# A plain group of chunks 8 to 11 opens the third batch, and ScalarE's queue loads q and k of the later rounds

## The chip, the core and the metric

The program runs on one core of a Trainium2 chip. The time is device time in microseconds (us), from the first to the last instruction of one execution; lower is better. Engines: TensorE (PE, with its weight loads PEld), VectorE (DVE), ScalarE (ACT), GpSimd (POOL) and SyncE (SP), which only issues transfers.

## What is computed

Eight batches of 576 tokens with 512 features go through three layers, all in float32. First linear attention with 8 heads of 64:

```python
q_s = softmax(q, over the head's 64 features)
k_s = softmax(k, over the 576 tokens)
x = q_s @ (k_s.T @ v)                      # per batch and head
```

Then a layer norm and a feed-forward layer with 2048 hidden values, `x + relu(norm(x) @ w_ch1) @ w_ch2`, and last a causal attention with four experts, of which each token uses two. The change touches the first two layers only.

## The kernel before

Everything is held with features on the partitions and tokens along the rows, in two halves of T = 288 tokens (h = 0, 1). TensorE multiplies in a rounded format, so every operand is split into a high and a low part (`split`: the high part by ScalarE, the remainder by VectorE), and a product takes three matmuls (high x high, high x low, low x high).

**Attention.** A *unit* is one pair of heads of one batch: 32 units, four per batch. `a_unit` runs one in six steps: the maxima of k and q (`km`, `sm`), the transposed maximum of k (`pkm`), the exponents (`ke` on ScalarE, `qe` on GpSimd), the transposes of q (`pq`), the product of k and v (`pkv`), and the result (`po`), copied to `xT`. Units run ahead of the feed-forward layer: while batch b is multiplied, the units of batch b + 1 are worked on. q and k of a unit live in two buffers each, so unit n + 2 is loaded when unit n has used its own: k behind `k_exp` (L495 on), q behind the second `q_scale` (L510 on), v behind `kv_product`, all by SyncE's queue.

**Feed-forward.** The 2048 hidden values are 16 chunks of 128 (f = 0 to 15); chunks 0 to 11 are multiplied in this phase, 12 to 15 later. Batches 0 and 1 run plain: `Step.first` multiplies one chunk (12 matmuls into `psh`), `high`/`low` take the relu into `hh`, and `Step.rest`, one step later, adds it into four sums (`acc`). From the third batch on (`FAST = 2`), the chunks go in three groups of four (`fast_group`, 0 to 3, 4 to 7, 8 to 11). The normalised input is cut into four blocks: b11 and b21 are the two halves of the features of the first half of the tokens, b12 and b22 those of the second half. Each group makes its products from seven blocks, b11, b22, b21 and four differences: t1 = b12 - b11, t2 = b22 - t1, t3 = b12 - b22, t4 = b21 - t2 (made by GpSimd, then split). `XORD` is the order in which the products use them. One product is 12 matmuls (`pa`, `pb`, `pc`), a group 84, against 96 in the plain form; after a group, `second` adds its four hidden chunks to the sums (96 matmuls). The weights of the seven products (`w_r`) come from a table in HBM (`w_d`) that is made during batch 1: `Sums` forms sums of weight blocks and stores them by ScalarE's queue, 5 stores for each of six pairs of chunks.

**What sets the order.** The loops hand work out in slots: a batch's steps or pieces are cut into a number of slots, and each slot calls some step of a unit (every `UNIT_GAP` slots a unit begins), of a norm (`NORM_AT`), of the blocks (`Mix.part`, `Mix.send` which stores a block for later) or of `Sums`. The tile framework then puts each engine's instructions in an order of its own by when it takes their inputs to be ready, and each engine and each queue runs its list strictly in that order. Each transfer also waits for an earlier one that used the same of eight semaphores.

In the last slots of batch 1, the norm of the third batch's two halves runs (`layer_norm`, sums `pmu` and `pvar`); then `first_space` and `last_space` give out buffers for the seven blocks and `hid` (hidden values), and the third batch starts with its first seven-product group.

## Time and profile before

| | |
|---|---|
| median of three runs | 1344.47 us (1344.16 to 1349.64) |
| profiled execution | 1343.84 us |
| its span | 1341.8 us |
| TensorE busy | 1295.0 us (97%) |
| VectorE, ScalarE, GpSimd busy | 979.2, 738.4, 403.0 us |

Times below are microseconds from the start of the span. Batch 1 is multiplied from about 160 to 247, the third batch from there to about 350, the following four batches in 86 to 87 us each, and the last batch of this phase to 793. `psh`, `acc`, `pa`, `pb`, `pc` are the sums in PSUM of the feed-forward layer, `pkm`, `pkv`, `pq`, `po` those of the attention units; `xm`, `xw_a`, `xw_b` hold the seven blocks; `xc` is the centred input. TensorE's granted clock is given as a share of its full speed of 2.4 GHz; the lower level is 1.2.

### The profile page before, as it was taken

How to read it: one execution, taken by the hardware profiler on the slowest of the kernel's cores; microseconds unless marked ns; L12 is line 12 of the kernel's file. 1: busy time of each engine (PE TensorE's matmuls, PEld its weight loads, DVE VectorE, ACT ScalarE, POOL GpSimd, SP SyncE). 2: the span in 40 equal slices, each digit the busy share in tenths (PEclk: the TensorE clock that was granted, in tenths of full speed). 3: DMA queues.
4: the chain of work that ended last, by engine and by line, in shares of the span. 5: the costliest groups of instructions: out<-in, count | busy, mean ns of one | idle time of the engine just before them, and what ended most of it. 6: DMA issues, size and time to landing. Idle time of an engine off the chain costs nothing.

```text
span 1341.8 us, 27486 instructions
## 1 busy us (share of the span) xinstructions
PE 1295.0 (97%) x9907; PEld 1244.7 (93%) x9907; DVE 979.2 (73%) x2776; ACT 738.4 (55%) x1884; POOL 403.0 (30%) x496
## 2 busy tenths in 40 slices
PE   6999999799999999999999999999999999999998
PEld 5789989699899998999999999999999999999996
DVE  6885766868869778787577457787777777777774
ACT  5875435545445554544445235656565665666665
POOL 6676245333233322342225002112121112121222
PEclk9999999799999999999999999999999999999999
DMA  9763377665756758656367224333323242333122
GB/s 238 225 210 102 114 236 259 219 178 185 243 181 224 219 197 261 201 200 184 127 248 234 72 72 134 91 102 86 107 76 106 80 107 94 91 107 91 45 50 74
DMA packets 173414, 203.52 MB, mean 152 GB/s; under 512 B 93152, under 2 KB 137696, under 8 KB 170976
## 3 DMA queue, kind: packets, MB, share of 16 engines
q1 hardware_dynamic: 150656, 164.80, 41.2%
q10 hardware_dynamic: 22624, 36.97, 7.6%
q8 instruction: 79, 1.29, 0.4%
q14 instruction: 55, 0.45, 0.1%
HBM read 140.13 MB, written 46.40 MB: 139 GB/s over the span
## 4 chain that ended last, share of the span: by engine, by line
PE 77%; DVE 9%; DMA 5%; ACT 2%; issue 1%; SPq 1%; POOL 0%; DVEq 0%; ACTq 0%; POOLq 0%
PE acc L191 18%; PE psh L191 11%; PE psqk L191 7%; PE psc L191 7%; PE pa L194 6%; PE pssc L191 4%; PE py L191 4%; PE pso L191 4%; PE psv L191 4%; PE pc L194 3%; PE pst L1842 3%; DMA q<-in_q_dram 2%; PE po L191 1%; PE pb L194 1%; DVE km L453 1%
## 5 line engine op out<-in xcount | busy, mean ns | idle before, releaser
L191 PE MATMUL psh<-xhl,w 128*128 128x288 f32 x1248 | 190.4, 300 | 1.3 <-DVE xhl L712 1.0
L191 PEld LDWEIGHTS psh<-xhl,w 128*128 128x128 f32 x1248 | 174.2, 190 | 4.0 <-DVE xhl L712 1.5
L1825 POOL TENSOR_SCALAR sm<-sm,st,lg 128x128 f32<-128x128 f32 (+3 forms) x128 | 81.8, 649 | 264.9 <-DVE lg L1742 63.0
L191 PE MATMUL acc<-xw_a,w 128*128 128x288 f32 x912 | 130.6, 297 | 3.2 <-DVE xT L1404 3.2
L191 PE MATMUL acc<-hid,w 128*128 128x288 f32 x912 | 128.0, 297 | 3.6 <-DVE tmp L1341 3.6
L191 PEld LDWEIGHTS acc<-hid,w 128*128 128x128 f32 x912 | 123.0, 188 | 5.0 <-DVE tmp L1341 4.5
L191 PEld LDWEIGHTS acc<-xw_a,w 128*128 128x128 f32 x912 | 123.4, 188 | 4.5 <-DVE xT L1404 4.2
L191 PE MATMUL psqk<-x,wqk 128*128 128x288 f32 x768 | 112.9, 297 | 0.4 <-DVE k L1645 0.4
L191 PEld LDWEIGHTS psqk<-x,wqk 128*128 128x128 f32 x768 | 105.1, 188 | 1.6 <-PE pst L1842 0.6
L191 PE MATMUL psc<-hb,w 128*128 128x288 f32 x672 | 100.2, 298 | 0.0
L1404 DVE TENSOR_TENSOR xT<-xT,acc 128x288 f32<-128x288 f32 x152 | 66.9, 445 | 40.0 <-PE acc L191 39.4
L1813 ACT ACTIVATE sm<-sm,st 128x128 f32<-128x128 f32 (+3 forms) x144 | 83.9, 584 | 20.9 <-DVE st L1805 19.3
L191 PE MATMUL acc<-hh,w 128*128 128x288 f32 x576 | 89.2, 303 | 3.8 <-ACT hh L806 2.2
L191 PEld LDWEIGHTS psc<-hb,w 128*128 128x128 f32 x672 | 92.1, 188 | 0.3
L191 PEld LDWEIGHTS acc<-hh,w 128*128 128x128 f32 x576 | 80.4, 190 | 6.4 <-ACT hh L806 2.9
L1866 ACT ACTIVATE aTh<-pst 128x128 fp32r<-128x128 f32 (+4 forms) x224 | 70.1, 333 | 23.2 <-PE pst L1842 10.6
L1867 DVE TENSOR_TENSOR aTl<-pst,aTh 128x384 fp32r<-128x384 f32 (+3 forms) x196 | 72.3, 381 | 11.4 <-ACT aTh L1866 9.1
L1805 DVE CUSTOM_DVE_ANT_0 sm<-pssc,mask 128x128 f32<-128x128 f32 (+2 forms) x144 | 67.9, 482 | 16.1 <-PE pssc L191 6.4
L514 POOL TENSOR_TENSOR qe<-q,sm 128x320 f32<-128x320 f32 x64 | 46.9, 752 | 86.4 <-PE pkv L558 43.4
L656 POOL TENSOR_TENSOR sq<-sq 128x288 f32<-128x288 f32 x42 | 37.8, 899 | 108.0 <-ACT sq L687 105.9
L194 PE MATMUL pa<-xw_a,w_r 128*128 128x288 f32 x408 | 64.7, 303 | 2.1 <-ACT xw_a L200 1.8
L194 PE MATMUL pa<-xm,w_r 128*128 128x288 f32 x408 | 63.6, 299 | 0.5 <-DVE xT L827 0.5
(257 smaller groups left out, 3095.6 us busy)
## 6 DMA issues: line engine op xcount, KB each, us to landing
w_r<-w_d SPq DMA_DIRECT2D x118, 512.0 KB, 4.9
wraw<-in_moe_w_ch_dram SPq DMA_DIRECT2D x32, 512.0 KB, 4.7
xhl<-xn_d SPq DMA_DIRECT2D x14, 1152.0 KB, 5.1
xp_d<-xT ACTq DMA_DIRECT2D x16, 576.0 KB, 4.2
k<-k SPq DMA_DIRECT2D x32, 288.0 KB, 3.5
k<-in_k_dram SPq DMA_DIRECT2D x32, 256.0 KB, 3.5
q<-in_q_dram SPq DMA_DIRECT2D x32, 256.0 KB, 4.0
out_dram<-ot SPq DMA_DIRECT2D x32, 256.0 KB, 2.0
```

Source lines behind the costliest of these rows:

```text
L191: nc.tensor.matmul(o, lhsT, rhs, start=start, stop=stop)
L194: nc.tensor.matmul(o, lhsT, rhs, start=start, stop=stop, skip_group_check=True)
L453: nc.vector.tensor_reduce(self.km, self.kt.rearrange("p j c d -> p j d c"), axis=AX.X, op=ALU.max)
L514: nc.gpsimd.tensor_tensor(self.qe[:, :, j, :], self.qt[:, j], self.sm[:, 2, j * NCH:(j + 1) * NCH, None].to_broadcast([P, NCH, D]), op=ALU ...
L656: nc.gpsimd.tensor_tensor(self.t, self.t, self.sq[:, c], op=ALU.add)
L1404: nc.vector.tensor_tensor(xs[:, c], xs[:, c], ps, op=ALU.add)
L1805: nc.vector.tensor_tensor_reduce(out=sm[:m, c0:c1], in0=o_, in1=msk, scale=1.0, scalar=3e38 if n == 0 else st[:m, j, 0:1], op0=ALU.add, op ...
L1813: nc.scalar.activation(sm[:m, :w], sm[:m, :w], AF.Exp, bias=st[:m, j, last:last + 1], scale=-1.0, accum_out=st[:m, j, 2:3])
L1825: nc.gpsimd.tensor_scalar(sm[:m, :w], sm[:m, :w], st[:m, j, 3:4], self.gate()[:, j:j + 1], op0=ALU.mult, op1=ALU.mult)
L1842: nc.tensor.transpose(pt[:kw, kb * m:kb * m + m], sm[:m, kb * P:kb * P + kw], ident[:m, :m])
L1866: nc.scalar.activation(oh, from_, AF.Copy)
L1867: nc.vector.tensor_tensor(ol, from_, raw(oh), op=ALU.subtract)
```

## The change

**The plain group.** The third batch begins with chunks 8 to 11 in the plain form (`first_pieces`): four pieces on b11 and b21, with the last step of batch 1 after the first of them, then one piece on b12 and b22, the sums of the first half, three more pieces, and the sums of the second half. The seven-product form follows for groups 0 and 1 (`place` numbers the groups anew). b11 and b21 are split in slots 33 and 34 of batch 1, b12, b22, t1, t2 and t3 in the first slots of the third batch, t4 in the middle of its first group. The buffers move: b11 and b21 share a tile `xm`, b12 and b22 the other, where t4 takes b12's place. The second half's norm is asked for 8 slots after the first's, in place of 6, `Sums` every 5 slots in place of 4, and the first `w_r` loads 12 slots later.

**q, k and v.** From the units of the third batch on (22 that load another), q and k of unit n + 2 are asked for after unit n's `q_turn`, by ScalarE's queue; v is asked for one step later, still by SyncE.

```diff
-    def load_qk(n):
+    def load_qk(n, eng):
         for nm in "kq":
-            load(n, nm)
+            load(n, nm, eng)
...
-        nc.sync.dma_start(out=t[:, :, :NIL, :].rearrange("p j c d -> p j (c d)"),
+        eng.dma_start(out=t[:, :, :NIL, :].rearrange("p j c d -> p j (c d)"),
...
             nc.scalar.activation(self.ke.rearrange("p c j d -> p j c d"), self.kt, AF.Exp)
-            if next_unit(self.n) >= 2 * NPR:
+            if self.early and next_unit(self.n) >= 2 * NPR:
                 load(next_unit(self.n), "k")
...
         u.q_turn()
         for piece in u.q_parts(0):
             piece()
+        if next_unit(n) >= 2 * NPR:
+            load_qk(next_unit(n), nc.scalar)
         yield
...
+        if next_unit(n) >= 2 * NPR:
+            load_v(next_unit(n))
...
-                slots.setdefault(t + (6 if b == FAST else NORM_GAP) * h + i, []).append(g)
+                slots.setdefault(t + NORM_GAP * h + i, []).append(g)
...
+    def first_pieces():
+
+        f0 = 4 * (NG - 1)
+        us = (hid0, [spare_hid[0]] + hid0[1:])
+        acc = []
+
+        def one(f, h):
+            ps = ps_m.tile([P, 512], F32, tag="m", name="psh")[:, :T] if len(acc) < 2 else bank("psh", len(acc) % 4)
+            acc.append(ps)
+            mm1_parts(ps, f, h)
+            u = us[h][f - f0]
+            relu_split(ps, u[:, 0], u[:, 1])
+
+        first = [(12, lambda f=f, h=h: one(f, h)) for h in range(NH) for f in range(f0, FSPLIT)]
+        sums = [second(FAST, f0, False, (h,), us) for h in range(NH)]
+        return (first[:1] + [(12, state["prev"].rest)] + first[1:2] + [(0, lambda: more_banks.extend([0, 1]))] + first[2:5] + sums[0] +
+                first[5:] + [(0, last_space), (0, lambda: mixes[FAST].part("t4"))] + sums[1])
...
-        for gr in range(NG):
-            out_ += fast_group(b, gr) + second(b, 4 * gr, gr == NG - 1 and b < LAST)
+        out_ = first_pieces() if b == FAST else []
+        ng = NG - (b == FAST)
+        for gr in range(ng):
+            out_ += fast_group(b, gr) + second(b, 4 * gr, gr == ng - 1 and b < LAST)
...
         if b == FAST:
-            for i, nm in enumerate(XORD[:4]):
-                add(t + 2 + i, lambda nm=nm: m.part(nm))
+            for i, nm in enumerate(("b11", "b21")):
+                add(t - 6 + i, lambda nm=nm: m.part(nm))
+            add(t + 2, m.fourth)
+            add(t + 2, m.send)
+            add(48, lambda: x_pair(("b12", "b22")))
+            for i, nm in enumerate(("b12", "b22", "t1", "t2", "t3")):
+                add(49 + i, lambda nm=nm: m.part(nm))
...
-    slots.setdefault(38, []).append(once(first_weights))
+    slots.setdefault(50, []).append(once(first_weights))
...
-            slots.setdefault(1 + 4 * p + i, []).append(pinned(piece))
+            slots.setdefault(1 + SUMS_GAP * p + i, []).append(pinned(piece))
```

TensorE's list at the end of batch 1, before. The rows begin with the last step's sums behind them; `pa` from `xm` is the product with b11, `pvar` the variance sums, `pc` from `xm` the product with t1, `pa` from `xw_a` the one with t2.

```order
L191 MATMUL pvar<-lnsum,mean_r 128x288
L467 MATMUL pkm_3090<-ident,km_3073 128x128
L194 MATMUL pa<-xm,w_r 128x288 x12
L191 MATMUL pvar<-lnsum,mean_r 128x288
L485 MATMUL pkm_3090<-ident,cm_3092 128x128
L467 MATMUL pkm_3243<-ident,km_3189 128x128
L558 MATMUL pkv_3219<-ident,qe_3121 128x128
L485 MATMUL pkm_3243<-ident,cm_3245 128x128
L191 MATMUL pkv_3219<-v_136,ke_3113 64x66 x10
L194 MATMUL pc<-xm,w_r 128x288 x2
L194 MATMUL pa<-xw_a,w_r 128x288 x2
```

TensorE's list at the same place now, behind the first plain piece (12 `psh` from `xm`, with both `pvar` among them, the second ahead of the last one) and the 12 matmuls of the last step. The first 36 matmuls of `psh` here are the pieces of chunks 9, 10 and 11 on the first half; the single `psh` behind `pkv` is the first that reads b12, and `acc` are the first half's sums.

```order
L192 MATMUL psh<-xm,w_6_592 128x288 x6
L486 MATMUL pkm_3079<-ident,cm_3081 128x128
L192 MATMUL psh<-xm,w_6_592 128x288 x6
L192 MATMUL acc<-xw_a,w_8_595 128x288 x3
L192 MATMUL psh<-xm,w_6_592 128x288 x20
L553 MATMUL pq_3125<-ident,qe_3107 128x112 x4
L192 MATMUL psh<-xm,w_6_592 128x288 x4
L559 MATMUL pkv_3179<-ident,qe_3107 128x128
L192 MATMUL pkv_3179<-v_136,ke_3102 64x66 x10
L192 MATMUL psh<-xm,w_6_592 128x288
L192 MATMUL acc<-xw_a,w_10_597 128x288
```

Before, four single transposes and one unit's k-v product stand between the second `pvar` and the first matmul on t1; now 52 matmuls of 288 columns stand between it and the first matmul on b12, with one unit's transposes and k-v product among them.

SyncE's list in batch 1, before: v of one unit, then k and q of the next, each two transfers.

```order
L416 DMA v_140<-in_v_dram 112x4x64 x2
L418 DMA v_140<-in_v_dram 128x2x64
L403 DMA k_2013<-in_k_dram 128x2x256
L405 DMA k_2013<-in_k_dram 128x2x64
L403 DMA q_2022<-in_q_dram 128x2x256
L405 DMA q_2022<-in_q_dram 128x2x64
```

ScalarE's list in batch 1 now (`w_d` from `w_0` are stores of `Sums`, `hh` a relu, `xT` a copy of a result, `ke` the exponent of an earlier k in the buffer that the next k takes).

```order
L1259 DMA w_d<-w_0_152 128x2x256 x2
L404 DMA q_2211<-in_q_dram 128x2x256
L406 DMA q_2211<-in_q_dram 128x2x64
L823 ACTIVATE hh<-psh 128x288
L603 ACTIVATE xT<-po_2169 128x288
L823 ACTIVATE hh<-psh 128x288
L499 ACTIVATE ke_2142<-k_1621 128x2x5x64
L404 DMA k_2208<-in_k_dram 128x2x256
L406 DMA k_2208<-in_k_dram 128x2x64
```

SyncE's list keeps the v transfers and the w_r loads alone; q stands ahead of the exponent that frees k's buffer, k behind it, and relus and copies stand between them on ScalarE.

## Rows read from the trace of the kernel before

**Rows 1.** The page: busy time, share of the span and instructions.

```profile
PE 1295.0 (97%) x9907; PEld 1244.7 (93%) x9907; DVE 979.2 (73%) x2776; ACT 738.4 (55%) x1884; POOL 403.0 (30%) x496
```

**Rows 2.** By stage: length, PE, PEld, DVE, ACT, POOL busy, clock, DMA share, GB/s.

```profile
250.00:300.00 50.00, 41.41 (x324) 39.23 (x321) 37.30 (x75) 24.78 (x56) 19.36 (x19) 0.86 0.71 212
165.00:350.00 185.00, 168.58 (x1324) 161.12 (x1322) 142.54 (x276) 88.33 (x194) 74.79 (x79) 0.95 0.67 217
437.00:523.00 86.00, 83.77 (x676) 81.12 (x675) 70.78 (x148) 44.26 (x101) 28.09 (x28) 1.00 0.66 209
```

**Rows 3.** By stage, in slices of ten microseconds; columns as in rows 2.

```profile
185.00:195.00 10.00, 7.84 (x43) 6.97 (x43) 6.36 (x15) 4.76 (x11) 3.20 (x5) 0.83 0.72 227
245.00:255.00 10.00, 4.53 (x39) 3.33 (x39) 9.96 (x21) 5.59 (x11) 4.23 (x5) 0.78 0.67 206
255.00:265.00 10.00, 6.91 (x30) 6.56 (x31) 8.56 (x10) 4.79 (x11) 5.00 (x3) 0.54 0.80 257
```

**Rows 4.** Timeline of TensorE: start, length, operation [idle before it, what ended that].

```profile
244.93 1.85 PE L194 MATMUL pa<-xm,w_r 128*128 128x288 f32 x12 [0.53 <-DVE xT L827]
246.62 0.29 PE L191 MATMUL pvar<-lnsum,mean_r 128*128 128x288 f32 x1
...
249.26 0.80 PE L191 MATMUL pkv<-v,ke 112*64 112x66 f32 x20 [0.24 <-ACT ke L498]
253.58 0.85 PE L194 MATMUL pc<-xm,w_r 128*128 128x288 f32 x2 [3.52 <-DMA q<-in_q_dram]
...
258.94 2.77 PE L194 MATMUL pc<-xm,w_r 128*128 128x288 f32 x10 [1.84 <-DVE xm L201]
261.50 2.60 PE L194 MATMUL pa<-xw_a,w_r 128*128 128x288 f32 x10
```

**Rows 5.** Timeline of VectorE: the splits of b21, b12, b22 and t1.

```profile
241.59 1.11 DVE L201 TENSOR_TENSOR xm<-xc,xm 128x576 fp32r<-128x576 f32 x1
...
253.43 1.48 DVE L201 TENSOR_TENSOR xw_b<-xc,xw_b 128x576 fp32r<-128x576 f32 x1
...
255.63 1.38 DVE L201 TENSOR_TENSOR xw_a<-xc,xw_a 128x576 fp32r<-128x576 f32 x1
256.93 1.95 DVE L201 TENSOR_TENSOR xm<-sq,xm 128x576 fp32r<-128x576 f32 x1
```

**Rows 6.** The chain of waits, 378 to 390: start, length, piece.

```profile
378.90 0.39 PE pq L552 x4
...
381.93 0.73 PE pkv L191 x20
...
386.84 1.60 PE pa L194 x12
```

**Rows 7.** Timelines of SyncE and VectorE, then all transfers of q.

```profile
175.60 0.37 SPq L403 DMA_DIRECT2D k<-in_k_dram  x1
...
176.58 0.42 SPq L403 DMA_DIRECT2D q<-in_q_dram  x1
...
182.23 0.82 DVE L457 TENSOR_REDUCE sm<-q 128x10 f32<-128x640 f32 x1 [2.78 <-DMA q<-in_q_dram]
...
DMA to landing us min/median/max: 2.5/3.9/6.7
```

**Rows 8.** Timelines of ScalarE and GpSimd: issues, and what stood behind them.

```profile
181.57 3.08 ACTq L1242 DMA_DIRECT2D w_d<-w  x2
186.04 0.31 ACT L581 ACTIVATE kv<-pkv,ks 64x64 fp32r<-64x64 f32 x1 [4.68 <-DMA w_d<-w]
...
252.89 1.41 POOL L764 TENSOR_TENSOR sq<-xc,sq 128x576 f32<-128x576 f32 x1
...
254.95 0.52 ACTq L787 DMA_DIRECT2D xn_d<-xw_b  x1
255.51 0.68 ACT L200 ACTIVATE xw_a<-sq 128x576 fp32r<-128x576 f32 x1 [1.99 <-DVE ks L576]
```

**Rows 9.** Waits of VectorE from 160 to 700: total, times, longest.

```profile
DVE sm L457 <- DMA q<-in_q_dram: 23.4, 13, 3.6
```

More of the change, by code (lines that the diff above doesn't have):

```diff
@@ L51 @@
 FAST = 2
+SUMS_GAP = 5
 XORD = ("b11", "t1", "t2", "b22", "t3", "b21", "t4")
@@ L569, in kv_product @@
                     mm(pkv[j * D:(j + 1) * D, :D + 2], self.ke[:kc, c, j], self.vt[:kc, c, j], c == 0, c == NIL)
-            if next_unit(self.n) >= 2 * NPR:
+            if self.early and next_unit(self.n) >= 2 * NPR:
                 load_v(next_unit(self.n))
@@ L748, in tile_kernel, with mm1_parts @@
     xslot, mixes = {}, {}
+    def mm1_parts(ps, f, h):
+        for c in range(NDC):
+            wh, wl = (w1s[f][:, i, c, :] for i in (0, 1))
+            x = xslot[(("b11", "b21"), ("b12", "b22"))[h][c // 2]]
+            mm(ps, wh, x[:, 0, c % 2], c == 0, False)
+            mm(ps, wh, x[:, 1, c % 2], False, False)
+            mm(ps, wl, x[:, 0, c % 2], False, c == NDC - 1)
     class Mix:
@@ L779, in part, with fourth @@
                 self.less("t3", "t3", "b22")
-            if nm == "b21":
+            if nm == "b21" and self.b != FAST:
                 self.at["t4"] = self.at["b21"]
                 self.less("t4", "t4", "t2")
+        def fourth(self):
+            self.at["t4"] = self.at["b21"]
+            self.less("t4", "t4", "t2")
         def send(self):
@@ L1281, in last_space @@
         later.append(mixp)
+        xslot["t4"] = xslot["b12"]
         xslot["b12"] = mixp.tile(XSL, F32R, tag="b12", name="xw_b")
@@ L1291, in last_space @@
             temps.extend([t[:, 0], t[:, 1]])
-        more_banks.extend([0, 1])
     class Stream:
@@ L1374, in plain_group @@
     def plain_group(b):
-        parts = (("b11", "b21"), ("b12", "b22"))
         def one(f, h):
@@ L1381, in one @@
             ps = bank("psh", (4 * (1 - h) + f) % 4)
-            for c in range(NDC):
-                wh, wl = (w1s[f][:, i, c, :] for i in (0, 1))
-                x = xslot[parts[h][c // 2]]
-                mm(ps, wh, x[:, 0, c % 2], c == 0, False)
-                mm(ps, wh, x[:, 1, c % 2], False, False)
-                mm(ps, wl, x[:, 0, c % 2], False, c == NDC - 1)
+            mm1_parts(ps, f, h)
             u = (hid0, hid1)[h][f - FSPLIT]
@@ L1391, in plain_group, with second @@
         return [(12, lambda f=f, h=h: one(f, h)) for h in (1, 0) for f in range(FSPLIT, NFC)]
-    def second(b, f0, final):
+    def second(b, f0, final, halves=(1, 0), us=None):
+        us = us or (hid0, hid1)
         def one(h, c):
@@ L1478, in tile_kernel @@
     begin(FAST + 1, slots, 4 * FSPLIT)
-    before_last = 7 * NG * (LAST - FAST)
+    before_last = 7 * place(LAST, 0)
     def first_weights():
@@ L1487, in first_weights @@
         stream.fill(-1)
-    slots.setdefault(38, []).append(once(first_weights))
+    slots.setdefault(50, []).append(once(first_weights))
     for p in range(FSPLIT // 2):
         for i, piece in enumerate(Sums(p).pieces()):
-            slots.setdefault(1 + 4 * p + i, []).append(pinned(piece))
-    n = 2 * HALF + HALF
-    slots.setdefault(2 * n + 1, []).insert(0, once(first_space))
+            slots.setdefault(1 + SUMS_GAP * p + i, []).append(pinned(piece))
+    slots.setdefault(4 * HALF + 1, []).insert(0, once(lambda: x_pair(("b11", "b21"))))
     run_steps(pass_(1, 0, FSPLIT), slots, wide)
-    last_space()
-    m = mixes[FAST]
-    m.part("b12")
-    state["prev"].rest()
-    for nm in ("b21", "t3", "t4"):
-        m.part(nm)
-    m.send()
+    own_space()
+    for n, gs in slots.items():
+        if n >= 4 * FSPLIT:
+            fronts[FAST + 1].setdefault(n - 4 * FSPLIT, [])[:0] = gs
     for b in range(FAST, B):
```

31 lines of the change are left out of this document (16 added, 15 removed).

## The prediction

> **What bounds the kernel now.** I read the busy shares first, then the time by stage, then the stage with the hole step by step. TensorE is busy for 97% of the span [rows 1], so a change gains only where TensorE waits or runs at its lower clock. Of the stages that the change touches, the steady batches leave little: in 437 to 523 us TensorE is busy for 83.8 of 86.0 us, and VectorE for 70.8 [rows 2]. From 165 to 350 TensorE is busy for 168.6 of 185 us, and 250 to 300 holds half of that loss: 41.4 us busy of 50, at a mean granted clock of 0.86 [rows 2]. In slices of ten microseconds the hole lies between 245 and 265: TensorE is busy for 4.5 and for 6.9 us, and the second slice has a granted clock of 0.54, so much of it ran at 1.2 GHz in place of 2.4 [rows 3]. A smaller loss stands in 185 to 195: 7.8 us busy, clock 0.83 [rows 3].
>
> The matmuls of the hole say why it is there [rows 4]. The third batch's first product (pa from b11) runs at 244.93. The second one reads t1, which needs the second half of the tokens (b12), whose variance sums (pvar) leave TensorE only at 246.62. From there the data must pass ScalarE, VectorE and GpSimd: VectorE finishes the split of b12 (xw_b) at 254.91, that of b22 at 257.01 and that of t1 (xm) at 258.88 [rows 5]; the product goes on at 258.94 [rows 4]. Between 246.75 and 264.10 TensorE did two blocks of twelve products (24 matmuls) and some 1.2 us of attention work. At full speed twelve matmuls of 288 columns take 1.60 us [rows 6], 0.133 us each, so 24 are 3.2 us; the 17.35 us held 4.4 us of work, and **12.9 us are lost**. Some 2.5 us of that is clock alone: the twenty matmuls from 258.94 to 264.10 filled 5.2 us [rows 4], where 20 cost 2.7 at the full clock.
>
> VectorE is what the hole waits for: it is busy throughout it. Yet b21's split, which opens no product in the old order until the sixth, was done by 242.70 [rows 5].
>
> **The change part by part, the plain group.** The third batch starts with chunks 8 to 11 by plain matmuls, and the seven-product groups follow for chunks 0 to 7. A plain group has 8 pieces of 12 matmuls, 96, where the seven-product group has 84. That adds 12 x 0.133 = **+1.6 us** of TensorE, on the path, since TensorE sets the end. It removes 6 copies on ScalarE, 6 additions on VectorE and 7 loads of w_r per such group; none of these is on the path, and I cost them at nothing.
>
> What it buys is cover. Its first four pieces need b11 and b21 alone. In the new order, behind the second pvar, stand 1 matmul of the first piece, 12 of the last step, 12 of the second piece, 3 sums, and 24 of the third and fourth pieces, before the first that reads b12. These are 52 x 0.133 = 6.9 us, and with the transposes of a unit's q (0.39) and its k-v product (0.73 [rows 6]), and two single transposes more, some 1.3 together, 8.2 us. Behind that, 45 matmuls of the first half's sums (6.0 us) stand between the pieces that need the second half. The need, from rows: from pvar at 246.62 b12 is ready 8.3 us later, b22 10.4 us later [rows 4, 5]. In the new VectorE order the column maximum of the next k, which stood ahead of these splits, stands behind them. So cover and need are about even. At worst the wait is the 10.4 us against 8.2 us plus seven matmuls, 1.3 us, and a lower clock behind it; the ends for what remains of the 12.9 us are 0 and 7 (half of it). I take 3, nearest to the steady batches' boundaries (2.2 us idle in the whole of 437 to 523 [rows 2]). The term is **-10 us** (-6 to -13).
>
> Does VectorE allow it? From 165 to 350 it is busy for 142.5 of 185 us [rows 2], 77%. If 11 us go, and the 6 additions, the share is 81%, and in 437 to 523 it is 82% with TensorE nearly full [rows 2]. So the work that filled the hole finds room. What comes late next is the second half's hidden values within the group, whose relu on ScalarE and VectorE now stands among the next batch's units.
>
> **Part two, norms and weight sums.** The second half's norm is asked for two slots later and the weight sums are spread over five slots in place of four. By the order of instructions pvar of the second half stands about where it did, so I cost this at zero. t1 to t4 are split later, but the first product of chunks 0 to 3 comes 204 matmuls (96 + 12 + 96), 27 us, into the batch, and the w_r loads of that group are covered by the same 27 us.
>
> **Part three, q and k by ScalarE's queue.** 88 transfers leave SyncE's queue (22 units of four). On SyncE q stands behind k, and k waits until the exponent of an earlier k has freed its buffer. At 175.60 k could be issued, at 176.58 q, and VectorE, which had reached q's maximum, sat idle 2.78 us until 182.23 [rows 7]. This happens 13 times between 160 and 700, 23.4 us of VectorE [rows 9]. In the new ScalarE order q is issued ahead of the exponent that k waits for, so this wait goes; what is late next is k, which still needs its buffer and lands 2.5 to 6.7 us after issue (q's own figures) [rows 7]. On the path little of it counts: TensorE was idle for 2.2 us in the worst steady batch [rows 2], and the loss at 185 to 195, some 3.5 us with its clock, is the one place where the chain of waits runs through that q. Ends: -3.5 for batch 1 and -4 for the four steady batches.
>
> Against it stands ScalarE's time. A DMA issue holds what is queued behind it: at 254.95 ScalarE issued a store for 0.52 us, and the activation behind it, whose data GpSimd had made by 254.30, began at 255.51 [rows 8]. Four issues per unit at 0.42 to 0.52 us are 1.7 to 2.1 us per unit, 37 to 46 us of ScalarE in all. ScalarE has room in the mean (44.3 of 86 us busy [rows 2]), but behind an issue wait relus and copies for which TensorE waits. A harder case is in the trace as well: in batch 1 two stores of weights took 3.08 us to issue and kept ScalarE idle for 4.68 us until 186.04 [rows 8]. In batch 1 q and k come on top of 30 such stores. So batch 1 runs from -3.5 to +4.7; I take **-2**, since the q wait goes for certain and the sums are thinner. In the steady batches from -4 to +9 (four issues at each of five batch boundaries, 20 x 0.47); I take **+1**.
>
> One rule of the Trainium skill speaks against this part. The page "DMA: Bandwidth & Descriptors", section "Issuing engines are not separate DMA queues", says that transfers from whichever queue share the same 16 DMA engines, and that issuing from several saves only the issuing time, usually small beside the transfer. By it q would arrive only some 0.9 us sooner, and this part would come to about +1 us in place of -1. The rows say otherwise in one respect: what q lost was not issuing time alone but its place behind k.
>
> **The sum.** -10 + 1.6 - 2 + 1 = -9.4 us. The profiled execution took 1343.84 us (span 1341.8 and 2.0 around it), so 1334.4; the median of the three runs is 1344.47, 0.6 above it. I predict **1335 us**.
>
> **The rivals.** *The hole is only half filled.* VectorE, busy for nearly all of the hole, stays late: the splits of b12 and b22 and the four relus of the first half share it, and TensorE waits for the second half's hidden values instead. For it: VectorE's 82% in the steady batches goes with most of their idle time. Against it: 6.0 us of sums that need no second half. Then -5 + 1.6, and nothing from q and k: 1341 us.
>
> *ScalarE's queue becomes the wait* (the slower side). The issue of a k or q waits for its buffer, or for an earlier transfer, and behind it stand the relus on which the next sums depend. Nothing is gained once each of the 22 units costs TensorE 8.4 / 22 = 0.38 us; above 0.69 us a unit the kernel is slower by over 0.5%. At 0.8 us it loses 17.6 us against 8.4 gained: 1353 us. For it: the 4.68 us of batch 1 [rows 8]. Against it: in the steady batches ScalarE is half idle and waits there come from elsewhere.
>
> *The cover moves nothing*: the plain group waits for b11 and b21 as the old one did for t1. Then +1.6 and -1: 1345 us. Against it: b21's split was done at 242.70, 2.2 us before the old first product began [rows 4, 5].
>
> **How the numbers follow.** My forecast, from 1325 to 1338, has 0.60; the half-filled hole 0.21; ScalarE's queue 0.16, of which 0.05 stays within 0.5%; the last 0.03. A difference of 0.5% (6.7 us: below 1337.7 and above 1351.2) is about what a measurement of this kernel can tell from no change. So faster 0.60, the same 0.29, slower 0.11. The range is 1325 to 1348: below, all lower ends but one; above, the half-filled hole and a queue that costs some 0.6 us a unit.
>
> **What would show it.** In the changed kernel's trace TensorE should be busy for over 9 of 10 us in every slice between 240 and 275, with a granted clock of 1.00, and the matmuls named psh from xm should follow the last step with no gap over 1.5 us. VectorE's wait for q should fall from 23.4 us to under 8 between 160 and 700. The time from the second batch's last step to the third batch's store of xT should be some 8 us shorter; the steady batches should keep their 86 to 87 us. I am wrong if the steady batches grow by over 1 us each with ScalarE idle behind a DMA issue, or if the gap comes back inside the plain group with VectorE as releaser.

## The result, and the profile after

The changed kernel takes 1352.52 us (median of seven runs, 1350.72 to 1357.04) against 1344.21 (1339.84 to 1349.64): a ratio of 1.0066, with a 95% interval of 1.0049 to 1.0083. It is **slower by 8 us**, where 1335 was forecast. The profiled execution has a span of 1354.2 us against 1341.8.

The page of the changed kernel, busy time and share of the span, answers to [rows 1]:

```profile
PE 1305.7 (96%) x9919; PEld 1252.0 (92%) x9919; DVE 975.8 (72%) x2770; ACT 730.5 (54%) x1878; POOL 404.2 (30%) x496
```

The same kernel by stage: length, then PE, PEld, DVE, ACT and POOL busy, granted clock, DMA share, GB/s. These are the stretches of [rows 2] and the hole of [rows 3]:

```profile
250.00:300.00 50.00, 46.23 (x389) 43.15 (x387) 36.61 (x76) 24.81 (x59) 22.40 (x22) 1.00 0.57 177
165.00:350.00 185.00, 175.48 (x1394) 167.87 (x1394) 144.40 (x278) 87.83 (x198) 75.86 (x79) 0.99 0.64 210
437.00:523.00 86.00, 79.15 (x626) 76.74 (x625) 59.79 (x124) 38.80 (x91) 27.67 (x28) 0.96 0.61 193
...
245.00:255.00 10.00, 10.00 (x92) 9.74 (x91) 9.92 (x19) 5.90 (x13) 5.24 (x4) 1.00 0.53 171
255.00:265.00 10.00, 9.65 (x85) 8.92 (x83) 8.12 (x18) 4.24 (x9) 6.25 (x6) 1.00 0.45 137
265.00:275.00 10.00, 8.87 (x78) 8.11 (x73) 8.39 (x18) 4.34 (x11) 2.41 (x3) 1.00 0.42 111
...
470.00:480.00 10.00, 4.87 (x35) 4.40 (x34) 1.63 (x4) 1.93 (x6) 0.20 (x1) 0.88 0.81 291
480.00:490.00 10.00, 9.73 (x59) 9.73 (x60) 9.32 (x21) 6.25 (x15) 5.18 (x6) 0.78 0.33 107
```

The hole is filled: 10.0 and 9.65 us busy at a clock of 1.00, where it was 4.5 and 6.9 at 0.78 and 0.54. (The slice behind it, 265 to 275, falls short of the nine tenths that were named, with 8.87.) But 437 to 523, where TensorE was busy for 83.8 of 86 us, now shows 79.2. The ends of the batches tell how this adds up. ScalarE stores the second half of xT when a batch is done; here are these stores from batch 1 on, first of the kernel before, then of the changed one (timeline of ScalarE: start, length):

```profile
246.37 0.52 ACTq L834 DMA_DIRECT2D xp_d<-xT  x1
...
350.19 0.53 ACTq L1411 DMA_DIRECT2D xp_d<-xT  x1
...
435.23 0.53 ACTq L1411 DMA_DIRECT2D xp_d<-xT  x1
...
522.91 0.52 ACTq L1411 DMA_DIRECT2D xp_d<-xT  x1
...
608.82 0.53 ACTq L1411 DMA_DIRECT2D xp_d<-xT  x1
```

```profile
246.87 0.52 ACTq L851 DMA_DIRECT2D xp_d<-xT  x1
...
343.95 0.52 ACTq L1425 DMA_DIRECT2D xp_d<-xT  x1
...
434.95 0.52 ACTq L1425 DMA_DIRECT2D xp_d<-xT  x1
...
530.62 0.52 ACTq L1425 DMA_DIRECT2D xp_d<-xT  x1
...
620.99 0.52 ACTq L1425 DMA_DIRECT2D xp_d<-xT  x1
```

The third batch takes 97.1 us in place of 103.8 (-6.7). The three steady batches behind it take 91.0, 95.7 and 90.4 in place of 85.0, 87.7 and 85.9: **+18.4 us**. The gain is there, and the steady batches lose nearly three times as much. Together that is 11.7 of the 12.4 us between the two spans. (The fourth of the steady batches, to the stores at 690.71 and 700.87, takes 79.9 in place of 81.9, so the four that the prediction speaks of lose 16.4.)

The waits of the changed kernel from 160 to 700 us (total, times, longest) name the place. The first line answers to [rows 9], 23.4 us in 13 times; `tmp` are the copies of the seven products, `kv` the scaled products of k and v. In the kernel before TensorE waited for no tmp or kv of VectorE by more than 2 us at a time:

```profile
DVE sm L458 <- DMA q<-in_q_dram: 30.8, 10, 7.4
...
PE pb L195 <- DVE tmp L1360: 9.5, 3, 5.3
...
PE po L192 <- DVE kv L586: 3.7, 3, 1.9
```

One such case in the timeline of all engines (a start, a length, and in brackets the idle time before it with what ended that):

```profile
468.63 6.70 SPq L1328 DMA_DIRECT2D w_r<-w_d  x5
...
469.67 0.37 ACTq L404 DMA_DIRECT2D q<-in_q_dram  x1
...
470.14 0.68 ACTq L406 DMA_DIRECT2D q<-in_q_dram  x1
...
471.21 0.29 DVE L586 SCALAR_TENSOR_TENSOR kv<-pkv,ks,kv 64x64 fp32r<-64x64 f32 x1 [0.49 <-ACT kv L582]
...
473.23 1.75 PE L195 MATMUL pa<-xw_a,w_r 128*128 128x288 f32 x12
478.90 0.82 DVE L458 TENSOR_REDUCE sm<-q 128x10 f32<-128x640 f32 x1 [7.40 <-DMA q<-in_q_dram]
479.76 0.82 DVE L1360 TENSOR_TENSOR tmp<-pc,tmp 128x288 f32<-128x288 f32 x2
...
480.27 2.05 PE L195 MATMUL pb<-xm,w_r 128*128 128x288 f32 x7 [5.29 <-DVE tmp L1360]
```

Read it from the top. SyncE, whose list no longer holds k and q, asks for five w_r of 512 KB from 468.63 on. One microsecond later ScalarE asks for q. VectorE reaches q's maximum (sm) at 471.50, 1.8 us after the request, and stands there for 7.4 us, because q lands only at 478.8. Behind it in VectorE's list wait the copies (tmp) of the seven products, and TensorE's next product (pb) waits 5.3 us for one. The wait costs more than its length, since the granted clock is down behind it: 0.88 and 0.78 in the two slices from 470 and 480 above, and in the whole list of TensorE the 12 matmuls of `pb` take 3.25 us where the 12 of `pa` ahead of the wait took 1.75. The chain of waits of this kernel shows the landing, counted from the request of q's second transfer, the one of 64 KB:

```profile
459.40 2.40 DMA q<-in_q_dram
...
470.14 8.64 DMA q<-in_q_dram
```

A q that meets no w_r lands in 2.4 us, this one in 8.6. Why does it meet them? Counted in the order of the requests, it is the q of unit 26, and ScalarE asks for it as soon as its buffer is free (GpSimd's `qe` of unit 24 ends at 469.64). In the kernel before, the q of unit 26 stood in SyncE's list behind the 14 w_r of the batch, and was asked for 37 us later:

```profile
468.09 36.45 SPq L1312 DMA_DIRECT2D w_r<-w_d  x14
...
506.52 0.41 SPq L403 DMA_DIRECT2D q<-in_q_dram  x1
```

The w_r themselves begin where they did, 36.1, 33.7 and 32.1 us into the three batches (at 380.07, 468.63 and 562.75) against 34.3, 32.9 and 35.2 before (384.53, 468.09 and 558.07). So it is q that came to them, and not they that ran ahead to q. What the DMA engines did from 455 to 482 us (40 slices of 0.68 us):

```profile
DMA  0000747493000000069699969999998999400000
GB/s 0 24 0 0 164 96 170 110 306 78 0 0 0 0 0 0 0 114 292 154 208 204 120 237 413 413 357 368 396 403 316 376 384 360 173 36 6 0 0 0
```

From 468 to 478 they are nearly full. This agrees with the rule of the Trainium skill that the prediction cited (page "DMA: Bandwidth & Descriptors", section "Issuing engines are not separate DMA queues": transfers of all queues run on the same 16 engines). The number beside it here is 8.6 us against 2.4. By that rule the part came to +1 us in the prediction; what stood behind the late q in VectorE's list was not in that price.

### The profile page after: what moved, and what is told of

It reads as the page before. It is cut to its first block, busy times and chain, and to the rows that moved or that the text cites. A ratio compares the mean times of both kernels' runs of the same rounds, so it can differ in the third digit from the quotient of the medians.

```text
span 1354.2 us, 27434 instructions
## 1 busy us (share of the span) xinstructions
PE 1305.7 (96%) x9919; PEld 1252.0 (92%) x9919; DVE 975.8 (72%) x2770; ACT 730.5 (54%) x1878; POOL 404.2 (30%) x496
## 4 chain that ended last, share of the span: by engine, by line
PE 68%; DVE 10%; DMA 8%; ACT 3%; issue 2%; POOL 2%; ACTq 1%; SPq 0%; DVEq 0%; POOLq 0%
PE acc L192 14%; PE psh L192 11%; PE psqk L192 7%; PE psc L192 7%; DMA q<-in_q_dram 5%; PE pssc L192 4%; PE pa L195 4%; PE py L192 4%; PE pso L192 4%; PE psv L192 4%; PE pst L1874 3%; PE pc L195 2%; PE pb L195 1%; DVE xw_a L202 1%; DVE xm L202 1%
## 5 line engine op out<-in xcount | busy, mean ns | idle before, releaser
L192 PE MATMUL psh<-xhl,w 128*128 128x288 f32 x1248 | 187.4, 298 | 1.3 <-DVE xhl L717 1.1
L192 PE MATMUL acc<-xw_a,w 128*128 128x288 f32 x948 | 136.4, 297 | 5.1 <-ACT q L480 2.0
L192 PEld LDWEIGHTS acc<-xw_a,w 128*128 128x128 f32 x948 | 129.0, 189 | 6.8 <-DVE xT L1418 3.2
L192 PE MATMUL acc<-hid,w 128*128 128x288 f32 x864 | 125.2, 302 | 1.9 <-DVE tmp L1360 1.9
L192 PEld LDWEIGHTS acc<-hid,w 128*128 128x128 f32 x864 | 119.7, 193 | 3.1 <-issue 2.1
L192 PE MATMUL psc<-hb,w 128*128 128x288 f32 x672 | 100.2, 298 | 0.0
L1898 ACT ACTIVATE aTh<-pst 128x128 fp32r<-128x128 f32 (+4 forms) x224 | 70.2, 333 | 23.4 <-PE pst L1874 11.0
L461 POOL TENSOR_TENSOR q<-q,sm 128x640 f32<-128x640 f32 x32 | 44.3, 1385 | 104.2 <-DVE sm L458 93.1
L661 POOL TENSOR_TENSOR sq<-sq 128x288 f32<-128x288 f32 x42 | 37.5, 893 | 103.8 <-ACT sq L692 101.7
```

The source lines that it names most:

```text
L192: nc.tensor.matmul(o, lhsT, rhs, start=start, stop=stop)
L461: nc.gpsimd.tensor_tensor(self.q3, self.q3, self.sm[:, 0, :, None].to_broadcast([P, 2 * NCH, D]), op=ALU.subtract)
L661: nc.gpsimd.tensor_tensor(self.t, self.t, self.sq[:, c], op=ALU.add)
L1898: nc.scalar.activation(oh, from_, AF.Copy)
```

## The experiments

Three accounts were to be told apart: the **queue** of k and q, the later **place** at which they are asked for, and the **plain group's** new order. All ratios are to the kernel before.

**Both parts, k and q on SyncE.**

```diff
-            load_qk(next_unit(n), nc.scalar)
+            load_qk(next_unit(n), nc.sync)
```

> The changed kernel with one word undone: q and k of units 10 to 31 are asked for at the same place of the program, but by SyncE's queue. Theory Q (the loss comes from handing these 88 transfers to ScalarE's queue): VectorE's wait for q between 160 and 800 us falls from 30.8 us to under 20, TensorE's waits for VectorE's tmp (9.5 us in three) go, and the time falls to 1335 to 1342 us, ratio to the kernel before 0.993 to 0.998. Rival P (the loss comes from the later place at which they are asked for, or from the plain group's new order): the time stays at 1348 to 1356 us, ratio 1.003 to 1.009, with the same waits.

Measured: 1339.8 us, 0.997 (0.9956 to 0.9985). VectorE's wait for q is 7.0 us. One word took back 12.7 us, so the queue carries the loss. But the kernel doesn't reach the forecast, and it has a wait, at 282 to 289 us, that the changed kernel doesn't have.

```profile
PE pa L195 <- DMA w_r<-w_d: 7.3, 1, 7.3
```

**The loads alone, no plain group** (the kernel before with the loads' part of the diff).

> The kernel before with the loads' part alone: q and k of units 10 to 31 asked for after the turned copies of q, by ScalarE's queue, and v one step later; no plain group. If the parts add up (theory Q or P, the loss being in the loads): the hole at 245 to 265 us stays and 5 to 15 us come on top, 1350 to 1360 us, ratio 1.004 to 1.012. If the loads cost nothing by themselves and the loss is the plain group's: 1342 to 1346 us, ratio 0.998 to 1.002.

Measured: 1336.08 us, 0.9938 (0.9921 to 0.9956). Neither case: the loads alone are *faster* by 8 us, with the hole left in. VectorE's wait for q falls from 23.4 to 15.1 us.

**The plain group alone** (the changed kernel with the loads at their old places, by SyncE).

> The changed kernel with the loads at the old three places and all by SyncE's queue: the plain group alone. If my term for the hole was right (-10 us for the hole, +1.6 us of it being already in): 1333 to 1338 us, ratio 0.992 to 0.996, with the stretch 240 to 270 us full. If the filled hole is given back by the new order in the later rounds: 1343 to 1352 us, ratio 0.999 to 1.006, with new waits of TensorE for VectorE between 270 and 800 us.

Measured: 1342.9 us, 0.9987 (0.9969 to 1.0005); just at the edge of the second expectation. The hole is gone, but TensorE is short of work again in the slices that follow, with a lower clock in the last (by stage, columns as above):

```profile
250.00:260.00 10.00, 8.24 (x64) 8.03 (x63) 9.94 (x16) 4.45 (x10) 8.04 (x6) 1.00 0.97 329
...
270.00:280.00 10.00, 8.18 (x76) 7.71 (x74) 7.12 (x15) 6.67 (x17) 4.13 (x5) 1.00 0.41 102
280.00:290.00 10.00, 7.64 (x46) 6.49 (x47) 4.99 (x14) 3.68 (x9) 4.18 (x5) 0.66 0.84 249
```

Its third batch (second store at 342.35, batch 1's at 239.86) takes 102.5 us against 103.8. What this kernel gained in its profiled execution (1337.0 us of span against 1341.8) stands ahead of that: batch 1's store is 6.5 us earlier. So the two parts don't add: -1.8 and -8 apart, +8 together.

**ScalarE's queue at the old places, with the plain group.**

> The changed kernel with the loads at the old three places (k after the exponential of k, q after the second scaling of q, v after the product of k and v), but k and q by ScalarE's queue. Theory Q: it loses as the changed kernel does, 1346 to 1356 us, ratio 1.002 to 1.009. Rival P (the place): it gains as the plain group alone, 1333 to 1340 us, ratio 0.992 to 0.997, since ScalarE's issues cost 0.4 to 0.5 us each beside other work.

Measured: 1355.57 us, 1.0078 (1.0056 to 1.01). With the plain group the queue loses at the old places too (0.9987 by SyncE there), so the place alone is not the cause. But it doesn't lose in the same stage, as the table at the end of this section shows: here 11.2 us of the 19.6 between the two spans stand before batch 1's store (251.02 against 239.86) and 5.3 in the steady batches. At the new place the queue costs 5.2 before that store (246.87 against 241.66) and 12.0 in the steady batches.

**q or k alone back on SyncE** (both parts, `load_qk` at its new place).

```diff
-            load(n, nm, eng)
+            load(n, nm, nc.sync if nm == "q" else eng)
```

> The changed kernel with q alone back on SyncE's queue, at the same place of the program; k stays with ScalarE. Theory B: q stands ahead of the w_r loads in SyncE's list again, lands in 3 to 4 us, VectorE's wait for q falls from 30.8 us to under 12, and the time falls to 1334 to 1342 us. Rival S, or that k is as much to blame: 1346 to 1354 us.

> The changed kernel with k alone back on SyncE's queue; q stays with ScalarE. Theory B: k's loads hold the w_r behind them only until k's exponential, which is before q is asked for, so the bursts still meet q: landings of 7 to 10 us stay and the time is 1346 to 1356 us. If instead the number of issues on ScalarE (44 fewer here) is the cause, half of the loss goes: 1343 to 1347 us.

Measured: with q on SyncE 1336.95 us, 0.9937 (0.9913 to 0.996), and VectorE's wait for q 2.1 us; with k on SyncE 1349.06 us, 1.0024 (1.0007 to 1.0041), and 18.9 us. It is q. One thing was not as expected: with q on SyncE it lands no sooner (median for its large part 6.0 us between 340 and 640, 5.7 in the changed kernel). What differs is when it is asked for, the q of unit 26 again behind the w_r, and when VectorE comes to it.

```profile
471.33 26.69 SPq L1328 DMA_DIRECT2D w_r<-w_d  x8
498.12 1.19 SPq L404 DMA_DIRECT2D q<-in_q_dram  x1
```

With both on SyncE that request stands at 500.26; with q on ScalarE it stands at 464.97 (k alone on SyncE) and 473.76 (the old places). With q on SyncE, k on ScalarE's queue rather helps (0.9937 against 0.997, the intervals just overlap).

**Half of each w_r, and its control.** From the second use of a tile on, only the first half of w_r is brought, in the changed kernel and in the kernel before. The other half of the tile then holds older weights, so these two only measure what the bytes cost.

```diff
-                nc.sync.dma_start(out=raw(t), in_=raw(w_d[...]))
+                s = (slice(None), 0) if any(m is t for m in self.got.values()) else (slice(None),)
+                nc.sync.dma_start(out=raw(t)[s], in_=raw(w_d[...])[s])
```

> The changed kernel with the later loads of the products' weights cut in half: from the second use of each w_r tile on, only its first half (256 of 512 KB) is brought, so the second half of the weights in it is an older one. Theory B (q, no longer ahead of the weights in one queue, shares the 16 DMA engines with bursts of five to eight w_r): the landings of q in the steady batches that took 8 to 10 us (444, 470, 563 us) fall to 4 to 6 us, VectorE's wait for q between 160 and 800 us from 30.8 us to under 15, and the time to 1340 to 1348 us. Rival S (ScalarE's queue itself, its issues or its order, is what makes q late): landings, waits and time stay, 1350 to 1356 us.

> Control for the halved w_r: the kernel before, with only the first half of each w_r tile brought from its second use on (the second half of those weights is an older one). Theory O: in the kernel before q is ahead of the w_r in SyncE's list, so halving gives back only the small waits for DMA, 1 to 7 us, 1337 to 1343 us, against the 25 us that it gave in the changed kernel. If halving the w_r gives 15 to 25 us here too (1319 to 1329 us), its gain in the changed kernel does not speak for the meeting of q and w_r.

Measured: 1327.3 us, 0.987 (0.9848 to 0.9893), for the changed kernel, and 1336.93 us, 0.994 (0.9922 to 0.9958), for the control. Halving gives 25 us in the one and 8 in the other, so some 17 us hang on the w_r of the changed kernel alone (1340 to 1348 us had been expected there). In the three steady batches halving gives 19.6 us (277.0 to 257.4) and 0.6 (258.6 to 258.0). VectorE's wait for q falls to 13.6 us there, and stays in the control (27.8 us). The control's 8 us, just past the range expected, say that the w_r cost something in the kernel before as well.

**v on ScalarE's queue too**, with the changed kernel, with q on SyncE, and without the plain group.

```diff
-            load_v(next_unit(n))
+            load_v(next_unit(n), nc.scalar)
```

> The changed kernel with v of the later units also asked for by ScalarE's queue (66 more transfers there), so that from unit 10 on SyncE's list holds the w_r loads alone and none of them stands behind a v that waits for its product. Theory B (bursts): the w_r are then asked for one by one as their tiles come free, no burst of five or more meets q, q lands in 3 to 6 us, VectorE's wait for q falls from 30.8 us to under 15, and the time falls to 1332 to 1342 us. Rival S (the issues on ScalarE cost): 66 more of them at 0.4 to 0.5 us make it slower still, 1356 to 1375 us.

> The changed kernel with q on SyncE's queue and k and v on ScalarE's. Theory B: q stands ahead of the w_r in one list, as in the run with q alone on SyncE (0.994), and the bursts behind v are gone as well: 1330 to 1337 us. If v on ScalarE costs by its issues or by waiting for the product of k and v in ScalarE's list: 1338 to 1350 us.

> The kernel before with the loads' part alone (0.994) and v on ScalarE's queue too; no plain group. Theory B: its waits for q at 359, 381 and 468 us (4.1, 3.5, 2.3 us) shrink to under 2 us each and the time falls by 2 to 6 us, to 1330 to 1334 us; the hole at 245 to 265 us stays. Rival S: 66 more issues make it slower, 1337 to 1350 us.

Measured: 1347.2 us, 1.0031 (1.001 to 1.0052); 1338.02 us, 0.9956 (0.9938 to 0.9975); 1341.21 us, 0.9987 (0.9967 to 1.0007). All three miss what was expected of the bursts. The timeline of the first says why: with nothing but w_r in its list, SyncE still asks for seven of them in a row, 31.3 us into the batch (the store before is at 520.94), and q still comes into it. What these w_r wait for is mostly TensorE, which still reads their tiles (`pa`, 47 times, 184.8 us in all between 300 and 700).

```profile
552.27 13.65 SPq L1328 DMA_DIRECT2D w_r<-w_d  x7
...
553.63 0.38 ACTq L404 DMA_DIRECT2D q<-in_q_dram  x1
...
560.63 0.82 DVE L458 TENSOR_REDUCE sm<-q 128x10 f32<-128x640 f32 x1 [4.72 <-DMA q<-in_q_dram]
```

So v did not make the bursts, and k and q had not held them back. On the other rival the first run is clear: 66 more issues on ScalarE made it 5 us faster than the changed kernel, so the price of issuing isn't what it lost by.

**The loads alone, q on SyncE.**

> The kernel before with the loads' part alone, q by SyncE's queue and k by ScalarE's; no plain group. If the loads' gain of 8 us without the plain group came from freeing SyncE's queue of q: it goes, 1341 to 1346 us. If it came from the later place at which k, q and v are asked for, or from k: it stays, 1333 to 1339 us.

Measured: 1331.65 us, 0.9908 (0.9881 to 0.9936), better than both kernels. Without the plain group too q seems better on SyncE, but the difference there is 4 us (0.9938 to 0.9908, and the intervals overlap), with it 17 (1.0066 to 0.9937). The timeline of the loads alone by ScalarE, at the place that answers to 468 to 479 above, shows one thing that may make the rest: the w_r begin 0.4 us *behind* q's second transfer, where the changed kernel has them 1.5 us ahead (and level with it at 380 and 563 us, where q takes 5.5 and 7.8 us to land).

```profile
463.68 0.46 ACTq L405 DMA_DIRECT2D q<-in_q_dram  x1
...
464.11 4.10 SPq L1316 DMA_DIRECT2D w_r<-w_d  x4
...
468.14 0.82 DVE L457 TENSOR_REDUCE sm<-q 128x10 f32<-128x640 f32 x1 [2.26 <-DMA q<-in_q_dram]
```

**Only q's small part on SyncE** (64 of 320 KB).

```diff
-        eng.dma_start(out=t[:, :, NIL, :], ...)
+        (nc.sync if nm == "q" else eng).dma_start(out=t[:, :, NIL, :], ...)
```

> The changed kernel with only the small part of q (64 KB of its 320 KB) back on SyncE's queue; the large part (256 KB) and k stay with ScalarE. The small part waits for the same tile as the large one, so SyncE's list cannot run ahead with w_r while q is not yet asked for. Theory O (order of issue): q lands in 3 to 6 us, TensorE's waits for pb of 5 us go, and the time falls to 1335 to 1343 us, ratio 0.993 to 0.999. Rival L (the large transfer on ScalarE's queue is slow by itself): landings of 7 to 10 us and the time stay, 1348 to 1356 us.

Measured: **1328.81 us, 0.9881 (0.986 to 0.9902)**, the fastest that brings all its weights, by more than was expected, and not in the way expected. The timeline shows the burst where it was, level with the large part of q:

```profile
455.65 0.40 ACTq L404 DMA_DIRECT2D q<-in_q_dram  x1
...
455.80 36.14 SPq L1328 DMA_DIRECT2D w_r<-w_d  x14
492.04 0.38 SPq L406 DMA_DIRECT2D q<-in_q_dram  x1
...
502.01 0.81 DVE L458 TENSOR_REDUCE sm<-q 128x10 f32<-128x640 f32 x1
```

SyncE's list doesn't hold the w_r back: it has the small part of this q (again unit 26) behind the 14 w_r, at 492.04, about where all of q is asked for with q on SyncE (498.12). So q isn't whole before, and the framework puts its maximum 10 us behind that, 46 us behind the request of the large part; the same happens to every fourth q. Nobody waits for it. VectorE's wait for q is 4.0 us in all, and TensorE has no wait over 2.1 us from 160 to 700. The steady batches take 85.0, 84.9 and 85.4 us.

**The maximum alone moved down VectorE's list.** k and q stay on ScalarE's queue; the maximum may not stand ahead of the last matmul that the program has written when it comes to it.

```diff
+    def pin_max(u):
+        n0 = len(traced())
+        pe = [i for i in traced() if i.engine == ENG.PE][-1:]
+        u.q_max()
+        if u.n >= 2 * NPR + 2:
+            for i in traced()[n0:]:
+                tc.add_manual_dep(i, pe[0].name, NOSYNC, reason="not earlier")
```

> The changed kernel, all of k and q on ScalarE's queue as there, with one instruction per unit tied: VectorE's maximum of q (units 10 and later) may not stand ahead of the last matmul that the program has written when it comes to it. In VectorE's list it moves 20 to 60 rows down. Theory V (in its list VectorE meets the maximum 1.7 to 3 us after q is asked for, and all else of VectorE stands behind it while q lands in 7 to 10 us): VectorE's wait for q between 160 and 800 us falls from 30.8 us to under 6, TensorE's waits of 5 us for tmp go, and the time falls to 1327 to 1338 us, ratio 0.988 to 0.996. Rival Q (ScalarE's queue or the meeting of q with the w_r costs by itself): 1345 to 1356 us.

Measured: 1345.25 us, 1.0 (0.9983 to 1.0017), at the edge of the rival's range. VectorE never waits for q any more, and 7 of the 24 us between the changed kernel and the fastest one are back. The steady batches, 87.7, 89.1 and 86.8 us (stores at 345.84, 433.50, 522.57, 609.34), get back 13.5 of the 21.8 us by which the changed kernel's exceed the fastest one's. But the moved maximum, here of every unit and not of every fourth, has a price, 4.6 us in batch 1 (from the store ahead of it to its own) and 5.1 behind the steady batches among it: VectorE now waits elsewhere, for ScalarE's copies of qT (14.3 us before this edit):

```profile
DVE qT L545 <- ACT qT L542: 45.8, 17, 5.2
```

**Why the filled hole gave so little.** Four runs, all with good loads: the fifth w_r, for which TensorE waited in the first experiment, by ScalarE's queue (on that experiment's kernel); the first w_r asked for as early as in the kernel before, and the old spacings of norm and weight sums (both on the kernel with q alone on SyncE); and the fastest loads without the plain group.

```diff
-                nc.sync.dma_start(out=raw(t), in_=raw(w_d[...]))
+                (nc.scalar if self.n == MIDB else nc.sync).dma_start(out=raw(t), in_=raw(w_d[...]))
...
-    slots.setdefault(50, []).append(once(first_weights))
+    slots.setdefault(38, []).append(once(first_weights))
...
-                slots.setdefault(t + NORM_GAP * h + i, []).append(g)
+                slots.setdefault(t + (6 if b == FAST else NORM_GAP) * h + i, []).append(g)
-SUMS_GAP = 5
+SUMS_GAP = 4
```

> Both parts with q and k on SyncE's queue (the first experiment's kernel, 0.997), and of the 98 w_r loads the fifth alone asked for by ScalarE's queue. There TensorE waited 7.3 us at 284 us for this load, which stood in SyncE's list behind k and q of a unit that was not yet ready. If that order is the cause, the wait goes and the time falls by 6 to 8 us, to 1331 to 1335 us, ratio 0.990 to 0.993. If something else is late there next (VectorE's tmp, v or q), the time stays at 1336 to 1341 us.

> Both parts with k on ScalarE's and q on SyncE's queue (0.994), with the first four w_r asked for in slot 38 of the second batch's pass, as in the kernel before, in place of slot 50. If the loss of 9 us that stands at 280 to 300 us in place of the hole comes from late w_r: 1329 to 1333 us. If it comes from the attention units there (TensorE waited 3.5 us for ScalarE's kv): 1335 to 1340 us.

> Both parts with k on ScalarE's and q on SyncE's queue (0.994), with the two spacings of the second batch's pass as in the kernel before: the layer norm's halves 6 slots apart in place of 8, the weights' sums every 4 slots in place of 5. I costed the changed spacings at nothing: 1334 to 1340 us. If they move the norm that the plain group waits for, the second variance comes 2 slots (1.6 to 3.2 us) earlier and the group's b12, b22 with it: 1330 to 1334 us.

> The kernel before with the loads' part alone, and q's small part on SyncE's queue as in the fastest run (1328.8 us with the plain group); no plain group, so the hole at 245 to 265 us stands. If the plain group is worth its hole when the loads are out of the way (12 us of the hole less 1.6 us of products and some 4 to 6 us of new waits at 280 to 300 us): 1332 to 1337 us, 4 to 8 us above that run. If the hole is given back whole, as with old loads: 1326 to 1331 us.

Measured: 1338.46 us, 0.9947 (0.9923 to 0.997): the wait of 7.3 us went, but the next w_r is late by 4.6 us and 1.3 us of the median came off. Asked for earlier: 1338.47 us, 0.9952 (0.9935 to 0.9969), no better than 0.9937 without that edit. The old spacings: 1330.66 us, 0.9902 (0.9875 to 0.9929) against 0.9937 (0.9913 to 0.996): probably better, but the intervals overlap. The fastest loads without the plain group: 1330.87 us, 0.9897 (0.9874 to 0.9919), against 0.9881 with it. In these two profiled executions the third batch takes 102.2 us without (stores at 243.88 and 346.11) and 93.9 with it (244.13 and 338.04): -8.3 us. 4.4 of this is left in the spans, and 2 in the medians, whose intervals overlap. The rest is lost in the last batch of this phase. From the store ahead of it to the first matmul of the third layer it takes 104.5 us with the plain group (673.56 to 778.03) and 100.2 without (681.92 to 782.14), and a good half of that lies in these 20 us (with the group first; columns as above):

```profile
693.56:713.56 20.00, 15.89 (x114) 14.90 (x113) 16.32 (x27) 14.66 (x32) 15.71 (x12) 1.00 0.82 280
```

```profile
701.92:721.92 20.00, 18.15 (x134) 17.47 (x132) 17.85 (x30) 14.29 (x31) 15.51 (x12) 1.00 0.86 285
```

Why the last batch is longer, no run shows.

**Where the time lies in these runs.** From the stores' starts as in the section on the result, one profiled execution each, in us: the second store of batch 1, the length of the third batch, of the three steady batches behind it, and the rest of the span.

| | batch 1 ends | third | three steady | rest |
|---|---|---|---|---|
| before | 246.4 | 103.8 | 258.6 | 733.0 |
| changed | 246.9 | 97.1 | 277.0 | 733.2 |
| k and q on SyncE | 241.7 | 98.7 | 265.0 | 732.6 |
| plain group alone, loads by SyncE | 239.9 | 102.5 | 261.1 | 733.5 |
| the same, k and q by ScalarE (old places) | 251.0 | 102.3 | 266.4 | 736.8 |
| q alone on SyncE | 242.2 | 100.0 | 257.7 | 738.1 |
| half of each w_r | 244.2 | 93.3 | 257.4 | 730.8 |
| its control, from before | 247.1 | 100.3 | 258.0 | 728.8 |
| q's small part on SyncE | 244.1 | 93.9 | 255.2 | 733.8 |
| the same, no plain group | 243.9 | 102.2 | 255.7 | 729.6 |
| maximum moved down | 248.8 | 97.0 | 263.5 | 738.3 |

**Batch 1.** With the plain group in, q on ScalarE's queue costs time in batch 1 as well (changed against k and q on SyncE; the old places against the plain group alone). The timelines of ScalarE and TensorE in the changed kernel show how:

```profile
170.52 2.94 ACTq L1259 DMA_DIRECT2D w_d<-w  x2
173.56 1.23 ACTq L404 DMA_DIRECT2D q<-in_q_dram  x1
176.39 0.38 ACTq L406 DMA_DIRECT2D q<-in_q_dram  x1
176.82 0.41 ACT L823 ACTIVATE hh<-psh 128x288 fp32r<-128x288 f32 x1 [6.01 <-POOL w_s L1243]
...
177.28 1.85 PE L192 MATMUL acc<-hh,w 128*128 128x288 f32 x12 [1.50 <-ACT hh L823]
```

Behind two stores of weights ScalarE asks for q; the second transfer of q goes out only at 176.39, when a v has landed (the chain of waits has that v up to 176.37), and the relu (`hh`) behind it starts 6.0 us after ScalarE's last work. TensorE waits 1.5 us for it, and is busy for 8.5 us of 170 to 180, where it is for 10.0 with k and q on SyncE.

## Why the prediction was wrong, step by step

**The hole (-10 + 1.6): right in place, near in size for its own batch.** Two of the three slices behave as named (10.0 and 9.65 us; the next has 8.87), and the third batch is 6.7 us shorter where "some 8 us" was forecast; with the loads out of the way it is 8.3. What the sum left out is that the batch's gain need not reach the end: with the old loads it was given back within the same batch (102.5 against 103.8 us), and even with the best ones 2 us remain in the medians, within the noise, since the last batch of the phase is 4.3 us longer. What gives it back there is not settled; nor is it behind the hole, where the last waits were for w_r in one run, and for w_r's successor in the next.

**Norm and sums at zero: open.** Taking the spacings back gave some 5 us (0.9937 to 0.9902), with overlapping intervals.

**q and k (-2 and +1): this step failed.** "This wait goes" was read from the row in which q stood behind k [rows 7]. The same list did something else that no row of waits names: it kept every fourth q behind the w_r of its batch, so that this q, and its maximum in VectorE's list with it, came when the w_r were through (506.52 in the kernel before, 500.26 and 498.12 with q back on SyncE). ScalarE asks for the same q at 469.67, one microsecond into the w_r, and shares the DMA engines with them. The wait for q grew from 23.4 to 30.8 us instead of falling under 8. And "on the path little of it counts" held for landings of 2.5 to 6.7 us [rows 7]; with landings of 5.5, 8.6 and 7.8 us, and q's maximum 1.7 to 1.8 us behind the request, VectorE, which takes its work in order, kept TensorE waiting (0.9, 5.3 and 3.3 us).

**The bound of +9 us for the four steady batches** was worked out from ScalarE's issuing time. They lost 16.4 (18.4 in the first three), by a mechanism outside that list. There the rival that came true is on the side named, and in the queue named, but not by its own means: TensorE waited for VectorE (9.5 us for `tmp`, 3.4 for `kv`), and 66 more issues on ScalarE cost nothing that shows. The sign "the steady batches grow by over 1 us each" came in three of the four, "with ScalarE idle behind a DMA issue" did not come with it.

**Batch 1 (-2).** Here the rival did come by its own means: ScalarE sat idle behind the issue of a q that waited for an earlier transfer, and TensorE behind ScalarE. Batch 1's store came 0.5 us later than before, and 5.2 later than with the same kernel by SyncE's queue. The range up to +4.7 had this in it; the value taken, with the wait for q gone "for certain", had not.

**The parts were summed as if independent.** Apart they give -1.8 and -8 us, together +8. q's queue costs 4 us without the plain group and 17 with it. In the traces the w_r begin up to 1.5 us ahead of q in the one order and 0.4 us behind it in the other; that this makes the difference is not shown, since no run changed this distance alone.

**What stays open.** That q on ScalarE's queue makes the loss is shown by exchanging q alone; that the w_r are its partner, by the halving against its control, which also reorders the lists. By the run with the maximum moved down, VectorE's wait for q accounts for 13.5 of 21.8 us in the steady batches. That the moment of q's request does it, and not the queue as such, is read from the traces; no run asked for q late by ScalarE's queue. What share of the rest is the order that the framework makes of all lists when a queue is changed, the runs don't tell.

## What to carry to other kernels

A load's place in a queue also sets which other transfers it meets: before moving it to another queue, ask what it stood behind in the old one, when the new one will ask for it, and how many bytes are then on their way. A queue whose engine also computes can pass the wait of a load on to that engine's own work. Where an engine works in order, look at how long after the request it comes to the load's first reader; a reader that isn't urgent belongs further down the list. Two edits that touch the same queue are measured apart and together.

## What the runs showed of the hardware that I had not expected

The two transfers of a q (256 and 64 KB) took 2.6 and 2.4 us to land with no w_r on the way, and 7.5 and 8.6 beside five transfers of 512 KB from another queue, while the DMA engines moved up to 413 GB/s. Moving a transfer of 64 KB per unit from one queue to another changed the time by 24 us (1.0066 to 0.9881). Every fourth of these transfers, and the maximum that needs it, then came some 30 us later, behind the w_r; no run shows how much of the 24 us this makes.
